# A chunked state recurrence with two token-mixing layers behind it: engine order of the recurrence written by hand, padded partitions, loads cut in pieces

## The chip, the cores and the metric

One core of one Trainium2 chip. The metric is the device time of one launch in microseconds, taken as the median of three runs; beside it stands one profiled execution with its own time.

## The reference, cut to what matters

Three layers run one after another. Only the first is touched here; the other two fill the second half of the time.

```python
B, H, S, D = 4, 8, 768, 40
state = zeros((B, H, D, D))
for t in range(S):
    y[:, :, t] = einsum('bhd,bhde->bhe', rt, state)
    Sa = einsum('bhde,bhe->bhd', state, at)
    state = state * wt[:, :, None, :] - einsum('bhd,bhe->bhde', Sa, bt)
    state = state + einsum('bhd,bhe->bhde', vt, kt)
x = y.transpose(0, 2, 1, 3).reshape(B, S, H * D)
x = moe(x)      # four causal attention experts, the best two of each token are mixed
out = moe2(x)   # a gated MLP with a matrix over the 768 tokens
```

All arithmetic is float32.

## The kernel before, in words

The 768 time steps are cut into 24 chunks of 32. `recurrence` handles one chunk per chain step `g`. Work on a chunk falls into three kinds.

Preparation, which doesn't depend on the state. `p_w(s)` is five VectorE operations on chunk `s`: a product scan of the decays (`pp`, L102), a reciprocal (L105), a scan backward (`rp`, L107), the scaled k and b (`kb`, L110) and the scaled a (`at`, L113); it ends with the load of chunk `s+3` (`load`, L85), since `xin` has three buffers. `p_t(s)` multiplies `kb` by `at` for two chunks at once on TensorE (L129) and VectorE masks the product out of PSUM (`ll`, L132). `p_x(s)` transposes `kb` on TensorE (L141, 8 operations) and ScalarE copies it out (`kbt`, L145).

Inversion, once for a unit of 2 or 4 chunks (`SIZES` = 2, 2, 4, 4, 4, 4, 4). `p_l` sends the masked products through memory into another layout (`lo`, L153, then `L`, L155), `p_sub` runs 31 pairs of VectorE operations on it (L168 and L170, each pair needs the one before), and `p_xt` sends the result back (`xo`, L176, then `xt`, L178). A unit has to be inverted before the first chain step of that unit can pass `f_u`.

The chain. Step `g` runs on TensorE `f_w` (L242, needs the state), `f_st` (state transposed, L287), `amat(g-1)` (L315), `f_kv` (L264), `f_u` (L253, needs `xt`), `ys(g-1)` (L332), `yk(g-1)` (L344, needs `am`), `f_s` (L272), `vt` (L297) and `f_lv(g+1)` (L235). VectorE adds to it `am` (L319), `xs` (L348) and the new state (L276, L280); ScalarE copies four results out of PSUM. The next `f_w` waits for L280.

What sets the order: the order of TensorE is that of the program text (`manual_schedule` names PE alone), and a table of numbers in `positions` says between which chain steps each piece of preparation is written. VectorE, ScalarE and the DMA queue of SyncE are ordered by a scheduler with its own estimate of times. PSUM tiles named `f` share two buffers (`FBQ = 2`); a tile takes a buffer when the reader of the last tile in it is done. They serve `p_t`, `p_x`, `f_st`, `amat`, `ys`/`yk` and `vt`.

Every load is one SyncE DMA (`xin` two): `xin` and `rv` have 104 partitions, two groups of 40 channels at partitions 0 and 64. The layers behind the recurrence (L394 on) and the preparation of their weights (`pre`) are the same in both kernels.

Of the kernel before, what the change touches and what calls it, by code (L numbers as in the profile page):

```python
# [23 lines left out]
AHEAD = 4.5  # L24
PPB = 11
RATB = 10
KTB = 11
FBQ = 2
PRQ = 2


def recurrence(ctx, tc, shape, x_in, rv_in, v_in, ident, store_x, pre=None):


    nc = tc.nc
# [7 lines left out]
    NW = NH * C  # L43

# [22 lines left out]
    ST = [cp.tile([Q, NH, 64], F32, name=f"ST{i}") for i in range(2)]
    U = [cp.tile([128, H, 64], F32, name=f"U{i}") for i in range(2)]
    for t in ST + U:
        nc.gpsimd.memset(t, 0.0)  # L70

    XIN, PP, AT, KBT, KB, LL, XT, RV, V = {}, {}, {}, {}, {}, {}, {}, {}, {}
    LX = {}
# [4 lines left out]
    def half(z, n=D):  # L78
        return slice(64 * z, 64 * z + n)

    def load(s):
        if s < NS:
            XIN[s] = ap.tile([Q, W + 3 * NW], F32, name="xin", bufs=3)
            for c0, c1 in ((0, W), (W, W + 3 * NW)):
                nc.sync.dma_start(XIN[s][:, c0:c1], x_in[s, :, c0:c1])  # L85

    def load_rv(g):
        if g < NS:
            RV[g] = cp.tile([Q, 4 * NW], F32, name="rv", bufs=2)
            nc.sync.dma_start(RV[g], rv_in[g])  # L90
# [6 lines left out]
    def p_w(s):  # L97

        xin = XIN[s]
        w = xin[:, :W]  # L100
        PP[s] = cp.tile([Q, NH, C + 1], F32, name="pp", bufs=PPB)
        nc.vector.tensor_tensor_scan(PP[s].rearrange("e n t -> e (n t)"), w[:, :W - 1],  # L102
                                     scan1.rearrange("e n t -> e (n t)"), 0.0, op0=OP.mult, op1=OP.add)
        inj = INJ[s % 2]
        nc.vector.reciprocal(inj[:, :, C:], PP[s][:, :, C:])  # L105
        rp = ap.tile([Q, NH, C + 1], F32, name="rp")
        nc.vector.tensor_tensor_scan(rp.rearrange("e n t -> e (n t)")[:, ::-1], w[:, 1:][:, ::-1],  # L107
                                     inj.rearrange("e n t -> e (n t)")[:, ::-1], 0.0, op0=OP.mult, op1=OP.add)
        KB[s] = ap.tile([Q, NH, 2, C], F32, name="kb", bufs=2)
        nc.vector.tensor_mul(KB[s], xin[:, W:W + 2 * NW].rearrange("e (n j t) -> e n j t", n=NH, j=2),  # L110
                             rp[:, :, None, 1:].to_broadcast([Q, NH, 2, C]))
        AT[s] = cp.tile([Q, NH, C], F32, name="at", bufs=RATB)
        nc.vector.tensor_mul(AT[s], xin[:, W + 2 * NW:].rearrange("e (n t) -> e n t", n=NH), PP[s][:, :, :C])  # L113
        load(s + 3)

    def p_t(s):

        k = unit_of[s]
        c = s - starts[k]
        if c == 0:  # L120
            LL[k] = cp.tile([128, 2, 4 * H, C], F32, name="ll", bufs=3)
        pt = ps.tile([128, 2, 512], F32, name="f", bufs=FBQ)
        pz = pt.rearrange("p z (c h t) -> p z c h t", c=2, h=H)
        for j in range(2):
            for h in range(H):
                for q2 in range(2):
                    for z in range(2):
                        n = 2 * h + q2
                        nc.tensor.matmul(pz[64 * q2:64 * q2 + 64, z, j, h],  # L129
                                         KB[s + j][half(z), n].rearrange("e j t -> e (j t)"), AT[s + j][half(z), n],  # L130
                                         start=(j == 0 and h == 0), stop=True, skip_group_check=True)
        nc.vector.tensor_mul(LL[k][:, :, c * H:(c + 2) * H], pt.rearrange("p z (n t) -> p z n t", t=C),  # L132
                             mask[:, None, None, :].to_broadcast([128, 2, 2 * H, C]))

    def p_x(s):

        KBT[s] = cp.tile([128, 2, H, D], F32, name="kbt", bufs=KTB)
        kb = KB[s].rearrange("e (h q) j t -> e h (q j t)", q=2)
        pt = ps.tile([128, 2, 512], F32, name="f", bufs=FBQ)
        for h in range(H):  # L140
            nc.tensor.transpose(pt[:, h // 4, h % 4 * Q:(h % 4 + 1) * Q], kb[:, h], ident[:Q, :Q])  # L141
        for g in range(2):
            src = pt[:, g, :4 * Q].rearrange("p (h e) -> p h e", h=4)
            for z in range(2):
                nc.scalar.copy(KBT[s][:, z, 4 * g:4 * g + 4], src[:, :, half(z)])  # L145

    def p_l(k):
# [4 lines left out]
        for q in range(4):  # L152
            nc.sync.dma_start(lo[q], LL[k][rows(q ^ 1), q % 2, :n])  # L153
        for q in range(4):
            nc.sync.dma_start(L[q * n:(q + 1) * n], lo[q].rearrange("j n t -> n j t"))  # L155
# [4 lines left out]
    def p_sub(k, j0, j1):  # L160
        L, X = LX[k]
        m_ = 4 * SIZES[k] * H
        L, X = L[:m_], X[:m_]
        for j in range(j0, j1):
# [5 lines left out]
            nc.vector.tensor_sub(X[:, :m, j + 1:], X[:, :m, j + 1:], tv)  # L170

    def p_xt(k):
# [7 lines left out]
    def positions(k):  # L180
        g, cs = starts[k], SIZES[k]
        steps = range(g, g + cs)
        if k == 0:
            at, l, sub, xt = [-100.0, -99.0], -98.5, (-90.0, -60.0), -59.0
        elif k == 1:
            at, l, sub, xt = [-98.0, -97.0], -96.5, (-2.0, 4.4), 4.5
        elif k == 2:
            at, l, sub, xt = [-20.0, -19.0, -1.9, 0.6], 1.1, (1.5, 10.2), 10.3
        elif k == 3:
            at, l, sub, xt = [2.6, 4.2, 5.9, 8.0], 11.4, (12.0, 22.0), 22.2  # L190
        else:
            at = [3 * (g - AHEAD - cs + c) for c in range(cs)]
            l, sub, xt = 3 * (g - 4.2), (3 * (g - 4.0), 3 * (g - 0.7)), 3 * (g - 0.6)
        out = []
        for c, s in enumerate(steps):
            out.append((at[c], p_w, s))
            if c % 2:
                out.append((at[c] + 0.3, p_t, s - 1))
            out.append((at[c] + 0.6 + (c + 1) % 2 * 0.05, p_x, s))
        out.append((l, p_l, k))  # L200
        for j in range(0, C - 1):
            out.append((sub[0] + (sub[1] - sub[0]) * j / (C - 1), p_sub, k, j, j + 1))
        out.append((xt, p_xt, k))
        return out

    when = sorted([x for k in range(len(SIZES)) for x in positions(k)], key=lambda x: x[0])

    def run_until(gap):
        while when and when[0][0] < gap:
            x = when.pop(0)  # L210
            x[1](*x[2:])

    order = ctx.enter_context(tc.manual_schedule(engines={mybir.EngineType.PE}))
    for s in range(3):
        load(s)
    load_v(0)
    load_rv(0)
    load_v(1)
    load_rv(1)
    run_until(0)  # L220

    QS = range(4)
    pw, wsb = {}, {}
    aq = {}
# [32 lines left out]
    def f_kv(g):  # L257
        aq["s"] = pS = ps.tile([128, 2, 512], F32, name="ps")
        flat = KBT[g].rearrange("p z h e -> p (z h e)")
        for h in range(H):  # L260
            for q in QS:
                z = q % 2
                n, o = (D, (H + h) * D) if z else (64, h * D)
                nc.tensor.matmul(pS[half(z, n), q // 2, h * D:(h + 1) * D], flat[rows(q), o:o + n], V[g][rows(q), h],  # L264
                                 start=(h == 0), stop=False, skip_group_check=True)

    def f_s(g):
        pS = aq["s"]
# [801 lines left out]
```

## Time and profile before

| what | us |
|---|---|
| median of three runs | 1202.46 (1192.55, 1202.46, 1209.99) |
| profiled execution, its own time | 1195.38 |
| its span, first to last instruction | 1193.3 |
| PE, DVE, ACT busy in the span | 899.8, 698.4, 379.7 |
| state of chunks 4, 8, 12, 16 complete | 214.7, 315.5, 420.4, 518.8 |
| first load of the second layer landed, end of the recurrence's part | about 654.5 |

PE is TensorE, PEld its weight loads, DVE VectorE, ACT ScalarE, SP or SPq SyncE and its DMA queue. A float32 matmul of the program appears as two matmuls and two weight loads in the trace. A wait named "issue" is time in which the engine waited for nothing that the profile shows.

### The profile page before, as it was taken

The page shows a single profiled execution, that of the slowest core. Times are in us where ns is not written, and L with a number is a line of the kernel's source. Part 1 is how long each engine was busy: PE and PEld are TensorE (multiplying, and loading weights), DVE is VectorE, ACT ScalarE, POOL GpSimd, SP SyncE. Part 2 cuts the span into 40 slices and gives each one's busy share as a digit, 9 for nine tenths or more (in the row PEclk, how much of TensorE's full clock was granted, in tenths as well). Part 3 has the DMA queues.
Part 4 walks back from the last instruction along what each step waited for, and adds up shares of the span by engine and source line. Part 5 has one row for each costly group of instructions (what it writes and reads, how often), then busy time and mean ns, then how long its engine had stood idle before and what let it go on. Part 6 is the DMA issues. An engine that isn't in the chain of part 4 may idle for free.

```text
span 1193.3 us, 38319 instructions
## 1 busy us (share of the span) xinstructions
PE 899.8 (75%) x17018; PEld 805.7 (68%) x17018; DVE 698.4 (59%) x1645; ACT 379.7 (32%) x1095; POOL 151.4 (13%) x278
## 2 busy tenths in 40 slices
PE   2354475776488377559897678789988998899988
PEld 2344464776477276548786556678987998799888
DVE  5788955626543842651111999786578556855650
ACT  1011011111111011101111568655565556555631
POOL 2000000000000000000000772012111211121131
PEclk9999999985555665655655679899999999999999
DMA  7645354535345233533332420100010001000000
GB/s 187 141 100 113 88 114 94 130 91 131 79 99 132 51 84 76 107 83 73 64 74 56 139 84 28 34 1 1 18 50 1 1 18 51 1 1 18 17 1 34
DMA packets 108462, 79.44 MB, mean 67 GB/s; under 512 B 88905, under 2 KB 95305, under 8 KB 105802
## 3 DMA queue, kind: packets, MB, share of 16 engines
q1 hardware_dynamic: 108298, 77.01, 27.8%
q8 instruction: 133, 2.18, 0.8%
q14 instruction: 31, 0.25, 0.1%
HBM read 62.83 MB, written 14.16 MB: 65 GB/s over the span
## 4 chain that ended last, share of the span: by engine, by line
PE 51%; DVE 27%; DMA 10%; issue 6%; ACT 4%; SPq 1%; POOL 1%; DVEq 0%; ACTq 0%; POOLq 0%
DVE sub L168 5%; DVE X L170 5%; DMA xin<-in_x_dram 5%; PE mm L827 5%; PE mm L828 4%; PE mm L829 4%; PE f L332 3%; PE f L315 3%; PE mp L786 3%; PE ps L264 3%; PE mp L716 2%; PE f L287 2%; PE pu L253 2%; PE f L344 2%; PE pw L242 2%
## 5 line engine op out<-in xcount | busy, mean ns | idle before, releaser
L141 PE MATMUL f<-ident,kb 104*128 104x104 f32 x192 | 38.0, 373 | 84.1 <-DVE ll L132 42.7
L168 DVE TENSOR_TENSOR sub<-X,L 128x31 f32<-128x31 f32 (+28 forms) x217 | 73.3, 338 | 44.1 <-DMA L<-lo 37.9
L141 PEld LDWEIGHTS f<-ident,kb 104*128 104x128 f32 x192 | 30.4, 213 | 87.0 <-DVE ll L132 43.6
L348 DVE TENSOR_TENSOR xs<-f,pp 104x512 f32<-104x512 f32 x24 | 16.6, 690 | 113.1 <-PE f L344 113.1
L756 ACT ACTIVATE f<-sc,nm 128x512 f32<-128x512 f32 (+3 forms) x128 | 68.9, 543 | 36.2 <-DVE nm L751 17.6
L477 DVE TENSOR_TENSOR ptl<-mp,pth 128x256 fp32r<-128x256 f32 (+2 forms) x144 | 65.4, 461 | 24.9 <-ACT pth L476 22.9
L170 DVE TENSOR_TENSOR X<-X,sub 128x31 f32<-128x31 f32 (+28 forms) x217 | 73.2, 337 | 6.2
L302 ACT COPY rv<-f 104x256 f32<-104x256 f32 x48 | 15.5, 375 | 192.4 <-PE f L297 187.3
L751 DVE TENSOR_REDUCE nm<-sc 128x1 f32<-128x512 f32 (+3 forms) x128 | 63.0, 502 | 23.4 <-PE sc L749 20.3
L319 DVE TENSOR_TENSOR am<-f,mask 128x512 f32<-128x512 f32 x24 | 16.5, 689 | 99.6 <-PE f L315 99.6
L145 ACT COPY kbt<-f 128x160 f32<-128x160 f32 x96 | 21.1, 307 | 165.7 <-PE f L141 165.7
L476 ACT CAST pth<-mp 128x256 fp32r<-128x256 f32 (+2 forms) x144 | 57.3, 410 | 35.1 <-PE mp L786 24.4
L786 PE MATMUL mp<-ident,f 128*128 128x128 f32 x336 | 61.0, 301 | 6.8 <-DVE ptl L477 3.8
L795 PE MATMUL pa<-pth,vv 128*128 128x256 f32 x192 | 55.8, 304 | 11.4 <-DVE at L807 8.2
L242 PE MATMUL pw<-ST,at 40*32 40x40 f32 x1536 | 30.3, 254 | 41.0 <-DVE ST L280 34.1
L129 PE MATMUL f<-at,kb 40*64 40x32 f32 x1536 | 47.4, 292 | 17.2 <-issue 14.2
L129 PEld LDWEIGHTS f<-at,kb 40*64 40x64 f32 x1536 | 45.1, 221 | 19.2 <-issue 15.8
L344 PE MATMUL f<-am,kbt 64*40 64x32 f32 x1536 | 36.9, 253 | 27.2 <-DVE am L319 23.6
L242 PEld LDWEIGHTS pw<-ST,at 40*32 40x32 f32 x1536 | 26.0, 154 | 46.1 <-DVE ST L280 36.1
L797 PE MATMUL pa<-ptl,vv 128*64 128x256 f32 x192 | 52.3, 294 | 2.2 <-DVE ptl L477 1.6
L344 PEld LDWEIGHTS f<-am,kbt 64*40 64x40 f32 x1536 | 32.9, 170 | 28.7 <-DVE am L319 24.1
L786 PEld LDWEIGHTS mp<-ident,f 128*128 128x128 f32 x336 | 43.8, 154 | 12.3 <-DVE f L772 4.1
(211 smaller groups left out, 2570.6 us busy)
## 6 DMA issues: line engine op xcount, KB each, us to landing
rv<-in_rv_dram SPq DMA_DIRECT2D x24, 832.0 KB
xin<-in_x_dram SPq DMA_DIRECT2D x24, 624.0 KB
xin<-in_x_dram SPq DMA_DIRECT2D x24, 214.9 KB
v<-in_v_dram SPq DMA_DIRECT2D x24, 160.0 KB
xd<-xs SPq DMA_DIRECT2D x96, 40.0 KB
out_dram<-ob SPq DMA_DIRECT2D x24, 160.0 KB
lo<-ll SPq DMA_DIRECT2D x20, 128.0 KB
L<-lo SPq DMA_DIRECT2D x20, 128.0 KB
```

The lines of the kernel that those rows point to most:

```text
L129: nc.tensor.matmul(pz[64 * q2:64 * q2 + 64, z, j, h], KB[s + j][half(z), n].rearrange("e j t -> e (j t)"), AT[s + j][half(z), n], start=(j ...
L141: nc.tensor.transpose(pt[:, h // 4, h % 4 * Q:(h % 4 + 1) * Q], kb[:, h], ident[:Q, :Q])
L168: nc.vector.tensor_mul(tv, X[:, :m, j:j + 1].to_broadcast([m_, m, n]), L[:, j:j + 1, j + 1:].to_broadcast([m_, m, n]))
L170: nc.vector.tensor_sub(X[:, :m, j + 1:], X[:, :m, j + 1:], tv)
L242: nc.tensor.matmul(pw[g][rows(q), h], AT[g][half(q % 2), n], ST[g % 2][half(q % 2), n, :D], start=False, stop=True, skip_group_check=True)
L344: nc.tensor.matmul(py[half(z), q2, c:c + C], KBT[g][64 * q2:64 * q2 + 64, z, 2 * p + h], am[64 * q2:64 * q2 + 64, h, z * HP + p], start=Fa ...
L476: nc.scalar.copy(hi, src)
L477: (lo_eng or nc.vector).tensor_sub(lo, src, hi.bitcast(F32))
L751: nc.vector.tensor_reduce(nm[:, z:z + 1], sc[:, :nn], op=OP.max, axis=AX.X, negate=True)
L756: nc.scalar.activation(pe[:, n0:n0 + nn], scs[z][:, :nn], AF.Exp, bias=nm[:, :1], accum_out=sm[:, z, i - i0:i - i0 + 1])
L786: nc.tensor.transpose(pp[:, j, z * 128:(z + 1) * 128], pes[z][:, (j0 + j) * 128:(j0 + j + 1) * 128], ident)
L827: nc.tensor.matmul(ps_, ah, bh, start=first, stop=False)
```

## The change

The order of VectorE and ScalarE is now that of the program text too, and the text is rewritten for it. `lazy(s)` holds the five VectorE operations of a chunk, `sub_parts(k)` the 31 pairs of a unit, `p_ll(s)` the masking, now of one chunk. `period(k)` lists the side work that is dealt out during the chain steps of unit `k`: the chunks of unit `k+2`, between them thirds of the pairs of unit `k+1`, each `p_ll` one chunk behind. In each chain step `fill` issues that list up to 52%, 86% and 100% of the step's share, at three places of VectorE's order: ahead of `am`, of `xs` and of the new state. TensorE's `p_t` and `p_x` come from a queue `pq` at two places of the step, after `yk` and after `f_lv`. The first four chunks and the pairs of unit 0 stand ahead of the chain, without anything between them.

The two channel groups are padded to 64 rows each, so `xin` and `rv` have 128 partitions; contractions over 40 rows become 64 rows with zeros, and the weights of `f_kv` are 40 columns wide where half were 64. `ps` is one tile for all steps, cleared once. Loads are cut: `xin` in four pieces, `rv` in four. ScalarE's copies of `kbt` and of the transposed state are two instead of four each.

Names in rows: `f`, `ps`, `pw`, `pu` are PSUM tiles, the number behind a name tells one tile from the next. VectorE before, in chain step g=3, where the pairs of unit 2 run, around that step's new state (`ST`):

```order
L348 TENSOR_TENSOR xs_2201<-f_2136,pp_252 104x512
L168 TENSOR_TENSOR sub_3224<-X_2319,L_2318 128x231
L102 SCALAR_TENSOR_TENSOR pp_2569<-xin_1533,scan1_86 104x528
L170 TENSOR_TENSOR X_2319<-X_2319,sub_3224 128x21x11
L105 RECIPROCAL INJ1_90<-pp_2569 104x16
L113 TENSOR_TENSOR at_2576<-xin_1533,pp_2569 104x512
L168 TENSOR_TENSOR sub_3227<-X_2319,L_2318 128x220
L107 SCALAR_TENSOR_TENSOR rp_2572<-xin_1533,INJ1_90 104x528
L170 TENSOR_TENSOR X_2319<-X_2319,sub_3227 128x22x10
L276 TENSOR_TENSOR ST0_93<-ps_2057,ST1_94 104x2x8x40
L110 TENSOR_TENSOR kb_2574<-xin_1533,rp_2572 104x1024
L168 TENSOR_TENSOR sub_3337<-X_2319,L_2318 128x207
```

VectorE now, in chain step g=5, from the new state on:

```order
L308 TENSOR_TENSOR ST0_124<-ps_132,ST1_125 128x2x8x40
L310 TENSOR_TENSOR ST0_124<-ST0_124,pp_724 128x2x8x40
L196 TENSOR_TENSOR sub_3206<-X_2302,L_2301 128x252
L198 TENSOR_TENSOR X_2302<-X_2302,sub_3206 128x18x14
L196 TENSOR_TENSOR sub_3209<-X_2302,L_2301 128x247
L198 TENSOR_TENSOR X_2302<-X_2302,sub_3209 128x19x13
L196 TENSOR_TENSOR sub_3212<-X_2302,L_2301 128x240
L198 TENSOR_TENSOR X_2302<-X_2302,sub_3212 128x20x12
L158 TENSOR_TENSOR ll_3215<-f_2565,mask_116 128x2x256
L118 SCALAR_TENSOR_TENSOR pp_3217<-xin_2249,scan1_111 128x528
```

The state stood inside a run of 62 pair operations and the next chunk's preparation; now three pairs stand between it and the mask of chunk 12 (`ll`, reading `f_2565`), and at most seven in a row anywhere in a four-step unit.

TensorE before, in chain step g=4, from `yk` on:

```order
L344 MATMUL f_2493<-am_2412,kbt_370 40x32 x32
L129 MATMUL f_2585<-at_2223,kb_2221 64x32 x32
L129 MATMUL f_2585<-at_2576,kb_2574 64x32 x32
L272 MATMUL ps_2414<-U0_95,kbt_496 40x40 x32
L297 MATMUL f_2690<-ident_60,U0_95 128x128 x4
L235 MATMUL pw_2697<-v_2262,ll_522 32x40 x32
L141 MATMUL f_2731<-ident_60,kb_2574 128x104 x8
L242 MATMUL pw_2697<-ST1_94,at_517 32x40 x32
```

TensorE now, at the same place of g=5; `f_2565`, the `p_t` product of the chunk before, was written one chain step earlier:

```order
L368 MATMUL f_2880<-am_2844,kbt_824 40x32 x32
L147 MATMUL f_2950<-at_2830,kb_2834 64x32 x32
L303 MATMUL ps_132<-U1_127,kbt_1134 40x40 x32
L325 MATMUL f_3035<-ident_60,U1_127 128x128 x4
L272 MATMUL pw_3042<-v_2654,ll_1000 32x40 x32
L170 MATMUL f_3076<-ident_60,kb_2834 128x104 x8
```

One chunk's `p_t` stands where two stood, and it takes a buffer of `f` while the one of the chunk before still holds another.

SyncE's queue at the start, from the eleventh row on, before:

```order
L85 DMA xin<-in_x_dram 104x529
L85 DMA xin<-in_x_dram 104x1536
L85 DMA xin<-in_x_dram 104x529
L85 DMA xin<-in_x_dram 104x1536
L85 DMA xin<-in_x_dram 104x529
L85 DMA xin<-in_x_dram 104x1536
L153 DMA lo_227<-ll 32x512 x4
L85 DMA xin<-in_x_dram 104x529
L85 DMA xin<-in_x_dram 104x1536
L155 DMA L<-lo_227 16x32x32 x4
```

And now, after the same three chunks, `v` and `rv`:

```order
L69 DMA xin<-in_x_dram 128x529
L69 DMA xin<-in_x_dram 128x512 x3
L69 DMA xin<-in_x_dram 128x529
L69 DMA xin<-in_x_dram 128x512 x3
L181 DMA lo_257<-ll 32x512 x4
L183 DMA L<-lo_257 16x32x32 x4
```

Two chunks instead of three stand ahead of `lo` of unit 0, and none between `lo` and `L`.

The diff, cut to its core:

```diff
-    def half(z, n=D):
+    def half(z, n=64):
-            XIN[s] = ap.tile([Q, W + 3 * NW], F32, name="xin", bufs=3)
-            for c0, c1 in ((0, W), (W, W + 3 * NW)):
+            XIN[s] = ap.tile([128, W + 3 * NW], F32, name="xin", bufs=3)
+            for c0, c1 in ((0, W), (W, W + NW), (W + NW, W + 2 * NW), (W + 2 * NW, W + 3 * NW)):
                 nc.sync.dma_start(XIN[s][:, c0:c1], x_in[s, :, c0:c1])
-            nc.sync.dma_start(RV[g], rv_in[g])
+            for c in range(4):
+                nc.sync.dma_start(RV[g][:, c * NW:(c + 1) * NW], rv_in[g, :, c * NW:(c + 1) * NW])
-    order = ctx.enter_context(tc.manual_schedule(engines={mybir.EngineType.PE}))
+    order = ctx.enter_context(tc.manual_schedule(engines={mybir.EngineType.PE, mybir.EngineType.DVE,
+                                                          mybir.EngineType.Activation}))
...
+    def period(k):
+        subs = sub_parts(k + 1) if k + 1 < len(SIZES) else []
+        steps = range(starts[k + 2], starts[k + 2] + SIZES[k + 2]) if k + 2 < len(SIZES) else []
+        out = []
+        n = max(len(steps) - 1, 1)
+        for i, s in enumerate(steps):
+            out += lazy(s)
+            out += subs[len(subs) * i // n:len(subs) * (i + 1) // n]
+            if i:
+                out.append((0.69, lambda s=s - 1: p_ll(s)))
+        if steps:
+            out.append((0.69, lambda s=steps[-1]: p_ll(s)))
+        else:
+            out += subs
+        return out
...
-                n, o = (D, (H + h) * D) if z else (64, h * D)
-                nc.tensor.matmul(pS[half(z, n), q // 2, h * D:(h + 1) * D], flat[rows(q), o:o + n], V[g][rows(q), h],
+                nc.tensor.matmul(pS[half(q % 2, D), q // 2, h * D:(h + 1) * D], KBT[g][rows(q), q % 2, h],
...
+        def fill(frac):
+            while dq and done[0] + dq[0][0] / 2 <= total * frac + 1e-6:
+                t, f = dq.pop(0)
+                done[0] += t
+                f()
+
+        for g in range(starts[k], starts[k] + SIZES[k]):
+            i = g - starts[k]
+            at = [(i + x) / SIZES[k] for x in SEG]
+            f_w(g)
+            f_st(g)
+            if g:
+                amat(g - 1)
+            if not last:
+                f_kv(g)
+            fill(at[0])
+            if g:
+                am(g - 1)
+            f_u(g)
+            if g:
+                ys(g - 1)
+                yk(g - 1)
+                load_rv(g + 1)
+            pe()
+            fill(at[1])
+            if g:
+                xs(g - 1)
+            if not last:
+                f_s(g)
+            load_v(g + 2)
+            vt(g)
+            f_lv(g + 1)
+            pe(1 if len(pq) < 3 else 2)
+            fill(at[2])
+            if not last:
+                state(g)
```

## Rows read from the trace of the kernel before

**Rows 1.** Stretches: busy time of PE, PEld, DVE, ACT, POOL; clock, DMA share, GB/s.

```profile
0.00:214.70 214.70, 99.60 (x2840) 89.31 (x2840) 153.61 (x325) 22.20 (x85) 10.52 (x26) 1.00 0.53 117
20.00:30.00 10.00, 0.00 (x0) 0.00 (x0) 1.71 (x3) 0.19 (x1) 0.00 (x0) 1.00 0.83 196
214.70:518.80 304.10, 204.96 (x7144) 184.93 (x7144) 155.26 (x316) 37.93 (x140) 3.87 (x10) 0.63 0.44 96
518.80:654.50 135.70, 115.28 (x4192) 104.34 (x4192) 25.76 (x40) 18.94 (x64) 0.00 (x0) 0.53 0.34 73
654.50:1193.30 538.80, 479.93 (x2842) 427.08 (x2842) 363.78 (x966) 300.65 (x806) 137.01 (x242) 0.93 0.09 28
```

**Rows 2.** What PE waited for, 214.7 to 518.8: total, times, longest.

```profile
PE f L344 <- DVE am L319: 18.4, 3, 8.1
PE pw L242 <- DVE ST L280: 16.8, 5, 5.4
PE f L141 <- DVE xs L348: 16.4, 2, 9.0
PE f L129 <- issue: 10.1, 6, 3.7
...
PE f L315 <- issue: 1.0, 2, 0.8
```

**Rows 3.** Timeline, all engines, 276 to 340 (start, length, idle before).

```profile
286.34 0.19 DVE L168 TENSOR_TENSOR sub<-X,L 128x31 f32<-128x31 f32 x1 [8.25 <-DMA L<-lo]
...
309.21 1.65 PE L141 MATMUL f<-ident,kb 104*128 104x104 f32 x8 [7.40 <-DVE xs L348]
...
314.63 0.82 DVE L280 TENSOR_TENSOR ST<-ST,pp 104x640 f32<-104x640 f32 x1
...
315.50 1.29 PE L242 MATMUL pw<-ST,at 40*32 40x40 f32 x64 [4.64 <-DVE ST L280]
```

**Rows 4.** Timeline of the start, 0 to 112.

```profile
0.79 2.71 SPq L85 DMA_DIRECT2D xin<-in_x_dram  x6
...
28.23 1.26 DVE L102 TENSOR_TENSOR_SCAN pp<-xin,scan 104x528 f32<-104x528 f32 x1 [8.86 <-DMA xin<-in_x_dram]
...
33.66 1.20 DVE L132 TENSOR_TENSOR ll<-f,mask 128x1024 f32<-128x1024 f32 x1
...
47.79 0.17 DVE L168 TENSOR_TENSOR sub<-X,L 64x31 f32<-64x31 f32 x1
```

**Rows 5.** Chain of waits, two stretches: start, length, what.

```profile
93.49 3.04 DMA xo<-X
96.55 5.74 DMA xt<-xo
...
275.56 6.86 DMA lo<-ll
282.44 3.78 DMA L<-lo
```

**Rows 6.** One stretch with the five VectorE operations of one chunk, columns of rows 1.

```profile
330.40:335.00 4.60, 1.73 (x63) 1.60 (x58) 4.44 (x5) 0.00 (x0) 0.00 (x0) 0.50 0.63 116
```

**Rows 7.** Costliest groups: line, engine, count, then busy and mean ns of one.

```profile
L168 DVE TENSOR_TENSOR sub<-X,L 128x31 f32<-128x31 f32 (+28 forms) x217 | 73.3, 338 | 44.1 <-DMA L<-lo 37.9
...
L170 DVE TENSOR_TENSOR X<-X,sub 128x31 f32<-128x31 f32 (+28 forms) x217 | 73.2, 337 | 6.2
...
L319 DVE TENSOR_TENSOR am<-f,mask 128x512 f32<-128x512 f32 x24 | 16.5, 689 | 99.6 <-PE f L315 99.6
```

**Rows 8.** Timeline of one chain step without side work, 549 to 586.

```profile
555.38 0.87 ACT L292 COPY s<-f 104x160 f32<-104x160 f32 x4 [1.07 <-PE f L287]
...
557.16 1.94 PE L264 MATMUL ps<-v,kbt 32*64 32x40 f32 x64
...
559.02 1.29 PE L253 MATMUL pu<-wsb,xt 32*32 32x40 f32 x64
```

**Rows 9.** Code fetches of 214.7 to 518.8: packets, MB, share of 16 engines.

```profile
q8 instruction: 56, 0.92, 1.4%
```

More of the change, by code (lines that the diff above doesn't have):

```diff
@@ L106, in p_w @@
[L106 to L111, printed above, removed]
@@ L176, in p_xt @@
         nc.sync.dma_start(xo.rearrange("q n l t -> (q n) (l t)"), LX[k][1][:4 * n].rearrange("n l t -> n (l t)"))
-        for q in range(4):
+        for q in QS:
             nc.sync.dma_start(XT[k][rows(q), :n], xo[q].rearrange("n l t -> l n t"))
[L180 to L190, printed above, removed]
-        else:
[L192 to L203, printed above, removed]
-        return out
@@ L206, in recurrence, with lazy, first @@
[L206 to L211, printed above, removed]
-    order = ctx.enter_context(tc.manual_schedule(engines={mybir.EngineType.PE}))
[L214 to L224, printed above, removed]
+    def lazy(s):
+        parts = []
+        def first():
+            parts.extend(w_parts(s))
+            parts[0][1]()
+        return [(1.25, first)] + [(t, lambda i=i: parts[i][1]()) for i, t in ((1, 0.9), (2, 1.25), (3, 1.22))]
@@ L353, in recurrence @@
     prep = None
     f_lv(0)
-    for g in range(NS):
-        last = g == NS - 1
-        f_w(g)
-        f_st(g)
-        amat(g - 1)
-        if not last:
-            f_kv(g)
-        run_until(3 * g + 1)
-        f_u(g)
-        ys(g - 1)
-        yk(g - 1)
-        load_rv(g + 1) if g else None
-        run_until(3 * g + 2)
-        if not last:
-            f_s(g)
-        load_v(g + 2)
-        vt(g)
-        f_lv(g + 1)
-        run_until(3 * g + 3)
-        if not any(x[1] in (p_w, p_t, p_x) for x in when) and prep_stack is not None:
+    for k in range(len(SIZES)):
+        dq = period(k)
+        total = sum(t for t, _ in dq)
+        done = [0.0]
+        def fill(frac):
+            while dq and done[0] + dq[0][0] / 2 <= total * frac + 1e-6:
+                t, f = dq.pop(0)
+                done[0] += t
+                f()
+        for g in range(starts[k], starts[k] + SIZES[k]):
+            i = g - starts[k]
+            at = [(i + x) / SIZES[k] for x in SEG]
+            last = g == NS - 1
+            f_w(g)
[25 more added lines that the diff above has]
+                state(g)
+            if prep is not None:
+                for _ in range(QPR):
+                    next(prep, None)
+        while dq:
+            dq.pop(0)[1]()
+        while pq:
+            pe()
+        if k == len(SIZES) - 3:
@@ L375, in recurrence @@
             prep_stack.close()
[L376 to L377 removed]
+        if k == len(SIZES) - 2:
             sub_stack.close()
[L379 removed]
             prep = pre() if pre is not None else None
[L381 to L383 removed]
     amat(NS - 1)
+    am(NS - 1)
     ys(NS - 1)
     yk(NS - 1)
+    xs(NS - 1)
     if prep is not None:
```

241 lines of the change are left out of this document (133 added, 108 removed).

## The prediction

> **What bounds the kernel now.** I read the stretches first, cut at the chain steps that complete a unit [rows 1]. Behind 654.5 us TensorE is busy 479.9 of 538.8 us; that code isn't touched, and I leave the stretch as it is. In the recurrence no engine is full: up to 214.7 VectorE works 153.6 us and TensorE 99.6; in the next twelve steps TensorE 205.0 of 304.1; in the last eight 115.3 of 135.7. So the gain has to come out of waits. Second view: what TensorE waited for in the twelve steps [rows 2]. `am`, the new state and `xs` cost 51.6 us in 10 waits, up to 9.0 each; nine rows of "issue", from 10.1 down to 1.0, add 40.7. Third, the timeline of one unit's worst step [rows 3]. VectorE takes up the pairs at 286.34 and stays with them; `xs` held back TensorE's next group by 7.4 us, the state is finished at 315.45 and `f_w` follows at 315.50. Those 29 us belong to one of four steps that take 101 together (304.1 / 3). Last, the start [rows 4]: VectorE has the product of chunks 0 and 1 to mask but was ordered to wait 8.86 us for chunk 3 first; `ll` runs at 33.66, the first pair at 47.79, and further chunks are mixed into the pairs, so the result leaves at 93.49 and lands at 102.29 [rows 5].
>
> **The start and the first four steps.** A chunk is 4.7 us of VectorE (4.44 in five operations and their gaps [rows 6]), an inversion 31 x (0.338 + 0.337) = 20.9 and 22.2 with gaps, `am`, `xs` or a one-chunk `ll` 0.69 each [rows 7], a state 1.65 (two of 0.82 [rows 3]).
>
> `lo` of unit 0 now leaves at about 18, but stands behind five chunks and two `rv`. Today the first part of chunk 3 is in at 28.2 [rows 4]; its rest and chunk 4, 1.5 MB at 196 GB/s, take 7.6 more, `lo` then 2.4 and `L` with its issue 5 (both estimates, from 6.86 and 3.78 under load [rows 5]): 43.2. This assumes that a load takes as long as now. Today's load rate is 196 GB/s with 0.83 of 16 engines busy [rows 1]. If that total is the limit, 128 rows for 104 cost 23% more time, and the pairs start at 52; if DMA cost nothing, VectorE's four chunks still hold them to about 24. I stay at 43.2, nearest to today's 47.79.
>
> On the engines, the busy share of 0.83 is nearly 13/16. [...] In the row six issues take 2.71 us while their data need more than ten [rows 4], so issue runs ahead of the data and I add nothing; in series, 16 further issues ahead of `lo` would add about 7 us.
>
> Then VectorE alone sets the pace. Unit 0's pairs run to 65.2. `xo` and `xt` take another 9 (3.04 + 5.74 [rows 5]), so `f_u(0)` can start at 74 instead of 102, and VectorE has the next unit's work meanwhile. The first two units hold two chain steps each and the side work of a four-chunk unit: twice 4 x 4.7 + 22.2 + 4 x 0.69 is 87.6; four states, three `am`, three `xs` are 10.7; together 98.3. Three waits are added, because VectorE is now strictly in order. At the end of each of the two units, the last `kb` has to go through TensorE's `p_t` and back before the two `ll` and the state behind them: TensorE has `p_x`, `f_s`, `vt`, `f_lv`, `p_t`, `p_x`, `p_t` to do after `xs`, and VectorE idles about 6 us, twice. And the first pair of unit 2 waits for `L`: the round trip from `ll` is about 11 (6.86 + 3.78 and an issue [rows 5]), of which VectorE has filled 6: 5 more. With 2.6 for handovers the sum is 65.2 + 98.3 + 12 + 5 + 2.6 = 183, against 214.7: **32 saved**.
>
> **The next twelve steps.** TensorE is the longer engine here (per unit 68.3 of work against VectorE's 51.8 [rows 1]). `f_kv` loses its wide weights: 1.94 becomes about 1.29, the same count with 32 columns [rows 8]; that is 2.5 per unit, 65.8 stay. The zero rows cost nothing: VectorE's time goes by columns (`am` on 128 rows and `xs` on 104 both took 0.69). What takes the place of the 17.2 us of VectorE waits per unit? I went through the new order of TensorE and VectorE by hand. With two `f` buffers a `p_t` product holds one until its `ll`, and `ll` is a whole chunk behind.
> - Second step: both buffers hold products. `vt` stands behind `f_s` and gets one when VectorE has done the state (1.65), three pairs (2.6) and `ll` (0.69): 4.9 us. Behind `vt` wait `f_lv`, `p_x` and the next `f_w`.
> - Fourth step: `f_st` waits for seven short pairs and `ll` behind the state (5.1); `p_t` and `f_w` cover all but 2.7.
> - With one buffer free, `amat` waits for ScalarE's copy of `f_st` (0.87 [rows 8]) in three steps, and `p_t` or `p_x` for `xs` in two: 2.7 + 1.8.
> - First step: `am` stands behind two pairs that wait for `L`, which lands 9 us into the step; `yk` is late by 2.2, `vt` by 0.5.
> - End of the unit: the last `ll` and the state take 2.5, `p_x` (1.65 [rows 3]) covers most: 0.9.
>
> That is 15.7, so the waits are spread more than removed. Handovers stay at 2.3 (101.4 less 68.3, 17.2 and 13.6). The issue waits are 13.6 per unit now. Code fetches (56 packets, 4.7 per step [rows 9]) go through the same DMA engines as the loads; a TensorE that waits for a buffer lets its code catch up, so I take 9.7, between nothing and 20. A unit: 65.8 + 15.7 + 2.3 + 9.7 = 93.5, three 280.5: **24 saved**. If `L` came 5 us later, the first step would lose those 5.
>
> **The last eight steps** have no `p_t`, no chunks, and the pairs of one unit only. `f_kv` gives 8 x 0.6 back, the wait for the last `L` takes about 2, and the weights of the second layer, now split at fixed places of VectorE's order, up to 3 when their load is late: 136. ScalarE's fewer, longer copies move the same columns: nothing.
>
> **Sum.** 183 + 280.5 + 136 + 538.8 = 1138.3 of span, 1140.4 with the 2.1 around it, against 1195.38 for the profiled execution. That execution lies 7.1 under the median of the runs; the same shift gives 1147.
>
> **Rivals.**
> 1. *More is hidden.* The buffer waits cover all code fetches and the loads run freer: three units of 83.8 (29 less) and a start 19 earlier: 1099. For it: a fetch that is late by up to 3.7 [rows 2] fits into a buffer wait of 4.9. Against: fetches fall late where loads are in flight, and loads now come closer together.
> 2. *The loads are bound by bytes.* 196 GB/s stays while `xin` and `rv` grow by 23%: the start is 9 later, `L` and `xt` come some 2 us later at six places, and issue waits grow to 17 per unit: 9 + 8 + 22 more, 1186. For it: the start's flat 196 GB/s. Against: 0.83 of the engines, so three hardly took part. The change would then not do what it says of the loads.
> 3. *Code fetch is slower, and the kernel with it.* [...] Price: 4.7 fetches a step over 20 steps is 94 fetches. Slower than before by 2%, 1226.5, needs 80 more than my sum, so 0.85 us more on each fetch; at 1 us it is 1241. For it: TensorE's issue waits of up to 3.7. Against: today's issue waits are 0.7 a fetch (40.7 / 56) with the DMA engines 0.44 busy; they would have to more than double.
>
> **How the numbers follow.** Forecast 0.57, with 1115 to 1178 as its own range (issue waits 0 to 20 per unit, pairs from 40 to 50); rival 1 0.22, rival 2 0.14, rival 3 0.07. A measurement tells about 2% from no change: 1178 and 1226. Faster: all of the forecast but its edge, and rival 1, 0.78; the same: mostly rival 2, 0.15; slower: rival 3, 0.07. The range, 1088 to 1190, leaves rival 3 and the outer ends out.
>
> **What would show it.** Right: `f_u(0)` near 74; the state of chunk 4 complete near 183, of chunk 16 near 464; no step of 35 us; in each four-step unit a `vt` that waits about 5 us for VectorE's `ll` and an `f_st` that waits about 3; VectorE idle for `L` at unit starts. Wrong: `vt` without a wait (then the units go towards 83), issue waits above 20 per unit, or the first pair after 50. If the part behind the recurrence differs from 538.8 by more than 10, the premise that it stays fails.

## The result, and the profile after

The changed kernel takes 1111.37 us, median of 4 runs (1109.5 to 1122.17), against 1201.22 for the kernel before, of 4 runs beside it: 0.927 of its time, 95% interval 0.918 to 0.936. The profiled execution takes 1109.5 us, with a span of 1107.8.

The stretches after, cut at the same chain steps as [rows 1] and with the same columns, and below them two pieces of 5 us:

```profile
0.00:165.10 165.10, 90.56 (x2832) 80.30 (x2832) 133.35 (x276) 19.35 (x49) 12.80 (x27) 0.66 0.55 158
165.10:433.20 268.10, 183.31 (x7152) 162.73 (x7152) 155.93 (x306) 36.09 (x96) 3.56 (x8) 0.65 0.49 129
433.20:569.00 135.80, 98.09 (x4192) 86.80 (x4192) 49.76 (x110) 18.02 (x48) 0.75 (x3) 0.70 0.41 97
569.00:1107.80 538.80, 480.06 (x2842) 427.24 (x2842) 365.52 (x966) 300.91 (x806) 138.32 (x242) 0.93 0.09 28
...
215.00:220.00 5.00, 4.16 (x217) 3.78 (x208) 0.98 (x2) 1.38 (x4) 0.00 (x0) 0.85 0.03 7
235.00:240.00 5.00, 4.16 (x124) 3.77 (x127) 1.58 (x3) 1.10 (x3) 1.11 (x2) 0.50 0.61 160
```

These rows show where the 85.5 us of span went: 49.6 from the start and the first four steps (214.7 to 165.1), 36.0 from the next twelve (304.1 to 268.1), nothing from the last eight (135.7, now 135.8) or behind. And a thing that the prediction did not have: TensorE does its matmuls in less busy time, 183.3 us in the twelve steps for 205.0 before, 98.1 in the last eight for 115.3, though these last still take as long. The zero rows make 18.5 and 16.0 us of that, as an experiment below shows; the narrower weights of `f_kv`, which the prediction had, belong to the rest. The granted clock there is 0.65 and 0.70; the clock records of this trace and of the one before hold two values alone, 0.5 and 1.0, called the low and the high level from here on. In the two short pieces TensorE is busy 4.16 us each, but runs 217 matmuls in the one and 124 in the other. The 1.00 of the first two lines of [rows 1] is no granted clock: the trace of the kernel before holds no clock record before 254.4 us, and the view prints 1.00 where there is none. The 64 matmuls of `f_kv` took 1.94 us there at 116.7, as they did at the low level in [rows 8]. The lines from 10 to 20 us further down have their 1.00 for the same reason.

What TensorE waited for in the twelve steps, answering to [rows 2] (total, times, longest):

```profile
PE f L325 <- DVE ll L158: 14.9, 3, 5.0
PE f L358 <- issue: 10.5, 8, 2.2
...
PE f L341 <- ACT s L320: 7.6, 9, 0.8
...
PE f L368 <- DVE am L347: 4.7, 1, 4.7
PE pw L279 <- DVE ST L310: 3.9, 3, 1.5
...
PE f L317 <- DVE ll L158: 1.2, 1, 1.2
```

Of the big waits for `am`, the state and `xs`, 51.6 us in all, one for `am` of 4.7 is left and small ones of up to 1.5; the largest is now `vt` (L325), once a unit. All waits for other engines add up to 37.4 us (51.6 before), all rows of "issue" to 47.2 (40.7 before). Four lines of the timeline answer to [rows 3] and [rows 4]: the first pair, `f_u(0)`, and twice the 64 matmuls of `amat`, once at the high and once at the low clock level.

```profile
30.49 0.18 DVE L196 TENSOR_TENSOR sub<-X,L 64x31 f32<-64x31 f32 x1 [0.40 <-DMA L<-lo]
...
58.57 0.31 PE L290 MATMUL pu<-wsb,xt 32*32 32x40 f32 x2 [20.11 <-DMA xt<-xo]
...
217.78 1.15 PE L341 MATMUL f<-rv 64*64 64x32 f32 x64 [0.84 <-ACT s L320]
...
237.25 1.96 PE L341 MATMUL f<-rv 64*64 64x32 f32 x64 [0.84 <-ACT s L320]
```

The start moved most: the first pair runs at 30.49 (47.79 before), because the chunks are there sooner.

What "issue" stands for can be read from the same trace, from the times of the 16 KB packets of the queue that the view calls `q8 instruction`, taken here for TensorE's code. Here are the next three issue waits of that stretch:

```profile
222.21 0.84 PE L358 MATMUL f<-rv,s 64*64 64x32 f32 x49 [1.46 <-issue]
...
227.03 1.16 PE L303 MATMUL ps<-U,kbt 32*40 32x40 f32 x52 [2.63 <-issue]
...
232.58 1.02 PE L147 MATMUL f<-at,kb 64*64 64x32 f32 x56 [1.95 <-issue]
```

Code packets landed at 220.83, 225.70 and 231.06, so TensorE went on 1.4, 1.3 and 1.5 us after each. In the twelve and the last eight steps all 37 issue waits over 1 us end 1.2 to 1.6 us after a code packet has landed; of the nine equally long waits for other engines, one does. So these issue waits are waits for code. The twelve steps have 14304 matmuls and weight loads on 56 packets, 255 to a packet.

### The profile page after: what moved, and what is told of

Read it like the earlier page. It is cut to its first block, busy times and chain, and to the rows that moved or that the text cites. A ratio compares the mean times of both kernels' runs of the same rounds, so it can differ in the third digit from the quotient of the medians.

```text
span 1107.8 us, 38413 instructions
## 1 busy us (share of the span) xinstructions
PE 852.0 (77%) x17018; PEld 757.1 (68%) x17018; DVE 704.5 (64%) x1657; ACT 374.4 (34%) x999; POOL 155.4 (14%) x279
## 4 chain that ended last, share of the span: by engine, by line
PE 53%; DVE 18%; issue 9%; ACT 5%; DMA 4%; SPq 1%; POOL 0%; ACTq 0%; DVEq 0%; POOLq 0%
PE mm L880 5%; PE mm L881 5%; PE mm L882 4%; PE mp L839 3%; PE f L341 3%; PE mp L769 2%; PE f L358 2%; PE f L317 2%; PE f L147 2%; PE ps L303 2%; PE pw L272 2%; PE f L368 2%; PE pw L279 2%; PE f L325 2%; PE f L170 2%
## 5 line engine op out<-in xcount | busy, mean ns | idle before, releaser
L196 DVE TENSOR_TENSOR sub<-X,L 128x87 f32<-128x87 f32 (+27 forms) x217 | 73.4, 338 | 33.4 <-DMA L<-lo 27.8
L198 DVE TENSOR_TENSOR X<-X,sub 128x87 f32<-128x87 f32 (+27 forms) x217 | 73.8, 340 | 7.4
L330 ACT COPY rv<-f 128x256 f32<-128x256 f32 x48 | 15.5, 375 | 175.7 <-PE f L325 159.3
L147 PE MATMUL f<-at,kb 64*64 64x32 f32 x1536 | 43.0, 272 | 30.2 <-DVE kb L133 13.8
L147 PEld LDWEIGHTS f<-at,kb 64*64 64x64 f32 x1536 | 39.4, 196 | 34.0 <-issue 11.5
L347 DVE TENSOR_TENSOR am<-f,mask 128x512 f32<-128x512 f32 x24 | 16.5, 689 | 69.9 <-PE f L341 69.9
L374 DVE TENSOR_TENSOR xs<-f,pp 104x512 f32<-104x512 f32 x24 | 16.5, 688 | 58.7 <-PE f L368 53.0
L172 ACT COPY kbt<-f 128x320 f32<-128x320 f32 x48 | 18.1, 429 | 99.4 <-PE f L170 99.4
L848 PEld LDWEIGHTS pa<-pth,vv 128*128 128x128 f32 x192 | 39.1, 203 | 17.2 <-DVE at L860 9.6
L290 PE MATMUL pu<-wsb,xt 32*32 32x40 f32 x1536 | 27.9, 231 | 29.6 <-DMA xt<-xo 22.2
L184 POOL MEMSET X<- 128x1024 f32 (+1 forms) x7 | 6.6, 951 | 312.9 <-DMA xo<-X 312.9
L292 ACT COPY U<-pu 128x320 f32<-128x320 f32 x24 | 10.2, 426 | 118.6 <-PE pu L290 118.6
```

Of the source, the lines that this page charges most:

```text
L147: nc.tensor.matmul(pt[64 * q2:64 * q2 + 64, z, h * C:(h + 1) * C], KB[s][half(z), n].rearrange("e j t -> e (j t)"), AT[s][half(z), n], sta ...
L196: nc.vector.tensor_mul(tv, X[:, :m, j:j + 1].to_broadcast([m_, m, n]), L[:, j:j + 1, j + 1:].to_broadcast([m_, m, n]))
L848: nc.tensor.matmul(pa[:, c0:], vv[:, j0 + j, e].rearrange("p a h -> p (a h)"), pth[:, j, c0:], start=(j0 + j == 0), stop=False, skip_group ...
```

## The experiments

My theory after the result was that order, loads and zero rows each carry a part: the order removes the long waits, 128-row loads arrive sooner, and the zero rows raise TensorE's clock, whose gain is given back as issue waits. The kernel before took medians of 1196 to 1199 beside these runs. Two versions that are 1% apart are not told apart by the 95% intervals of their ratios, which overlap; where the text leans on a difference of some 10 us, the four times of each don't overlap and the stretches of the profiled executions show it too. Where a kernel's stretches are shown, they are the twelve steps and the last eight, up to the last `xs` (133.9 us before, 133.7 after, counted so), with the columns of [rows 1].

**Two halves: the order alone, and all but the order.** The first is the changed kernel with the 104-row layout, products over 40 rows and whole loads:

```
-    C, Q = 32, 128
+    C, Q = 32, 104
-            XIN[s] = ap.tile([128, W + 3 * NW], F32, name="xin", bufs=3)
+            XIN[s] = ap.tile([Q, W + 3 * NW], F32, name="xin", bufs=3)
...
```

> The new order alone: 104 rows everywhere, products over 40 rows, whole loads, as in the kernel before. Theory A, order, loads and zero rows each carry a part: the first pair near 43 as foretold with loads as they were (12 us later than after the change), TensorE at the low clock, 1135 to 1145. Theory B, the order carries nearly all: 1111 to 1118. Theory C, loads and rows carry most: 1165 to 1190.

Measured: 1142.06 us (1135.18 to 1147.55), 0.956 of before (0.947 to 0.966); the first pair at 38.1, 5 us earlier than theory A has it, the state of chunk 4 at 181.8.

```profile
181.80:456.60 274.80, 203.37 (x7152) 181.22 (x7152) 156.27 (x307) 36.18 (x97) 3.54 (x8) 0.57 0.48 106
456.60:600.90 144.30, 111.98 (x4192) 100.26 (x4192) 49.85 (x110) 18.02 (x48) 0.75 (x3) 0.55 0.39 81
```

The other is the kernel before with 128 rows, products over 64 rows and loads in pieces:

```
-    C, Q = 32, 104
+    C, Q = 32, 128
-                                     KB[s + j][half(z), n].rearrange("e j t -> e (j t)"), AT[s + j][half(z), n],
+                                     KB[s + j][half(z, 64), n].rearrange("e j t -> e (j t)"), AT[s + j][half(z, 64), n],
...
```

> The kernel before with everything but the order: 128 rows, products over 64 rows, loads in pieces. Theory A, each carries a part: the granted clock rises above 0.5 in the recurrence, but the long waits for VectorE stay, 1170 to 1185. Theory B, the order carries nearly all: 1195 to 1203. Theory C, loads and rows carry most: 1130 to 1150.

Measured: 1164.02 us (1161.64 to 1170.39), 0.976 (0.967 to 0.984); the state of chunk 4 at 192.5. Its twelve steps, and its waits there:

```profile
192.50:493.00 300.50, 194.66 (x7144) 174.75 (x7144) 155.53 (x316) 38.15 (x140) 3.88 (x10) 0.60 0.43 111
...
PE f L345 <- DVE am L320: 21.0, 3, 8.0
PE f L142 <- DVE xs L349: 17.5, 2, 9.0
PE pw L243 <- DVE ST L281: 15.5, 4, 5.4
```

Theory A's time holds for the order alone; for this half its direction does, but 1164 lies 6 us under its range (and 14 above C's). The order is worth 57 us of 1199, all else 35, both together 88: they hardly overlap. By stretch, the start became 33 us shorter with the order alone, 22 with the rest and 50 with both, the twelve steps 29, 4 and 36. The waits of [rows 2] stay as they were without the new order (54 us), so it is the order that removes them. What this cut doesn't part: the narrow weights of `f_kv`, ScalarE's merged copies and the `p_t` of one chunk went with the order.

**The zero rows.** Products over 40 rows, all else as after the change:

```
-                                     KB[s][half(z), n].rearrange("e j t -> e (j t)"), AT[s][half(z), n],
+                                     KB[s][half(z, D), n].rearrange("e j t -> e (j t)"), AT[s][half(z, D), n],
...
```

> The changed kernel with the matrix products over 40 rows as before (each half of 64 without its 24 zero rows); loads, layout and order stay. Theory A, the zero rows raise the granted clock of TensorE: in the 268 us of twelve steps the clock goes from 0.65 back towards 0.50 and TensorE's busy time from 183 up to about 200, in the last eight steps from 98 to about 115; since part of that time is spent on issue waits today, the kernel loses 8 to 20 us, 1120 to 1131. Theory B, the denser order raises the clock: clock and busy time stay, 1111 within 5.

Measured: 1115.16 us (1113.94 to 1117.32), 0.935 (0.925 to 0.944).

```profile
166.20:433.30 267.10, 201.77 (x7152) 179.84 (x7152) 156.02 (x307) 36.08 (x96) 3.55 (x8) 0.56 0.49 129
433.30:567.60 134.30, 114.14 (x4192) 102.09 (x4192) 49.76 (x110) 18.02 (x48) 0.75 (x3) 0.54 0.41 97
```

The mechanism of theory A is there, its price is not. The clock falls to 0.56 and 0.54 and TensorE's work grows by 18.5 and 16.0 us; the stretches take as long as with zero rows. What gives way are the issue waits: 30.2 us in the twelve steps for 47.2, 16.3 in the last eight for 31.6; those over 1 us are 20 for 37, and all 20 end 1.2 to 1.7 us after a code packet. So with the loads in pieces the clock's gain is given back almost whole, to waits for code. With whole loads it is not quite so:

> Loads whole, of 128 rows, with products over 40 rows: between the order alone (1142) and whole loads with 64 rows (1100). Theory A, the gain between these two comes from the loads' 128 rows, and the clock's share is taken back by issue waits: 1100 to 1108, TensorE at the low clock (0.54 in the last eight steps, busy 112 to 114). Theory B, it is the clock's: 1125 to 1140.

(The edits of this run are those of the run above and the next one together.) Measured: 1111.8 us (1106.1 to 1113.59), 0.927 (0.922 to 0.933).

```profile
165.20:432.10 266.90, 195.62 (x7152) 173.86 (x7152) 155.97 (x306) 36.06 (x96) 3.09 (x7) 0.58 0.47 128
432.10:565.50 133.40, 114.46 (x4192) 102.32 (x4192) 49.80 (x111) 18.01 (x48) 1.04 (x4) 0.53 0.39 99
```

The time lies 4 us above theory A's range and 13 under B's; A's clock and busy time hold within 1 us. Against the order alone the 128 rows of the loads give 30 us (1142 to 1112), or 26 against the other version with loads of 104 rows below (1137.56), some 16 of them in the start (state of chunk 4 at 165.2 for 181.8). The products over 64 rows give another 11 (1112 to 1100, next run): 30 us less of TensorE's work shorten the twelve and the last eight steps by 14. Theory A's ordering holds.

**The pieces.** Loads whole, of 128 rows:

```
-            for c0, c1 in ((0, W), (W, W + NW), (W + NW, W + 2 * NW), (W + 2 * NW, W + 3 * NW)):
+            for c0, c1 in ((0, W), (W, W + 3 * NW)):
...
-            for c in range(4):
-                nc.sync.dma_start(RV[g][:, c * NW:(c + 1) * NW], rv_in[g, :, c * NW:(c + 1) * NW])
+            nc.sync.dma_start(RV[g], rv_in[g])
```

> The changed kernel with its loads whole again: a chunk in two pieces and r, v in one, of 128 rows. Theory A, the pieces bring the faster start: the first pair goes from 30.5 back to about 37 and the kernel loses 5 to 8 us. Theory B, the 128 rows (16 engines) alone do it: first pair at 30 to 32, 1111 within 4.

Measured: 1100.31 us (1099.36 to 1102.4), 0.922 (0.915 to 0.929): faster than the changed kernel, which neither theory had. The first pair runs at 28.96, so theory B's start holds.

```profile
168.80:427.30 258.50, 185.97 (x7152) 164.69 (x7152) 156.27 (x306) 36.11 (x97) 3.53 (x8) 0.64 0.47 129
427.30:555.50 128.20, 94.23 (x4192) 83.34 (x4192) 49.75 (x110) 18.03 (x48) 0.76 (x3) 0.73 0.40 102
```

The pieces cost 11 us in all: 9.6 and 5.5 in the later stretches, where 8 and 3 us of issue waits go with them. Up to chunk 4 they look 3.7 us better (165.1 for 168.8), but four other versions with whole loads take 162.6 to 167.3 to there, so no gain is shown; the first pair is 1.5 later with pieces, since `lo` is issued at 19.58 for 16.77. With products over 40 rows the pieces cost only 3 us (1115.16 to 1111.8, above) and the stretches are alike, so this price belongs to the faster TensorE.

> The changed kernel with only r, v whole (one load of 1 MB for four of 256 KB); the chunks stay in four pieces. Theory A, the pieces of r, v cost: the last eight steps take 128 as with all loads whole and not 133.7, the twelve steps 258 to 262, and the start stays at 165: 1096 to 1101. Theory B, the chunks' pieces cost: 1107 to 1113.

Measured: 1103.79 us (1099.3 to 1104.34), 0.921 (0.915 to 0.926); the twelve steps take 263.1, the last eight 128.7, the start 166.2. Nearer to theory A, 3 us above its range: r and v hold most of the price. Why pieces of 256 KB cost stays open: a code packet takes 0.98 us (median of the two stretches) with pieces as with whole loads.

**The wait for `ll`.** On top of whole loads, `ll` is masked right behind the next chunk's operations:

```
             out += lazy(s)
+            if i:
+                out.append((0.69, lambda s=s - 1: p_ll(s)))
             out += subs[len(subs) * i // n:len(subs) * (i + 1) // n]
-            if i:
-                out.append((0.69, lambda s=s - 1: p_ll(s)))
```

> Whole loads, and besides each chunk's ll is masked right behind the next chunk's five operations, before the pairs, so that a buffer f comes free about 2.6 us to 17 us earlier. Theory A, the wait of vt and f_st for ll (14.9 and 2.6 us in the twelve steps) is on the path: it goes, the twelve steps take 258.5 less about 13, the kernel 1100 less 10 to 15. Theory B, the supply of instructions paces TensorE: the waits for ll go, and the issue waits grow from 39 by as much; the kernel stays within 4 of 1100.

Measured: 1089.84 us (1085.81 to 1092.86), 0.911 (0.904 to 0.917); the twelve steps take 249.9. Its largest waits there:

```profile
PE ps L302 <- issue: 13.5, 5, 4.3
PE f L357 <- issue: 11.6, 7, 3.4
PE f L367 <- issue: 8.2, 5, 2.9
```

Both theories have a part. The `vt` wait is gone (2.7 us for `ll` are left, at `amat`) and waits for other engines fall by 17.5 us (32.3 to 14.8), but issue waits grow by 12 (39.2 to 51.1): of a removed wait about half reaches the time (258.5 to 249.9).

**Code supply.** First whether the loads delay it:

```
+        if 12 <= g < NS:
+            RV[g] = RV[g - 2]
-        if g < NS:
+        elif g < NS:
```

> Whole loads, but from chunk 12 on r and v aren't loaded: the tiles of two chunks before are used again, so these chunks' outputs are computed from other r and v. About 12 MB of loads less, most of them beside the last eight steps. Theory A, code fetches are late because loads stand in the same queues: in the last eight steps the issue waits go from 28 to under 12, the steps from 15 to 17 us to 13 to 14, the kernel is 12 to 20 faster than 1100. Theory B, a fetch has a pace of its own of about 3.3 us: issue waits stay above 22, steps at 15 to 16, the kernel within 6 of 1100.

Measured: 1092.34 us (1089.2 to 1095.05), 0.912 (0.907 to 0.917).

```profile
427.60:549.00 121.40, 92.60 (x4192) 81.38 (x4192) 49.72 (x110) 18.01 (x48) 0.75 (x3) 0.75 0.24 47
```

Traffic is halved (47 GB/s for 102), issue waits are still 24.8 for 28.3, steps 14.0 to 16.5. Nearer to theory B, with 2 us more gain than it allows. From the start times of the instruction queue's 16 KB packets, the shortest interval between two code fetches in the last eight steps is 3.34 us after the change, 3.28 with whole loads and 3.33 here: less traffic leaves it where it was. In the changed kernel's trace a packet takes a median 0.98 us, TensorE goes on no sooner than 1.19 after it has landed, and no packet starts sooner than 1.06 after such a restart: by estimate 3.2 in all, if each leads to the next. Then with fewer instructions, on whole loads and early `ll`. V and U share a tile, so that one product over 64 rows does what `f_kv` and `f_s` did:

```
-            V[g] = cp.tile([128, H, D], F32, name="v", bufs=2)
+            V[g] = cp.tile([128, 2, H, D], F32, name="v", bufs=2)
...
+            for q in QS:
+                nc.scalar.copy(V[g][rows(q ^ 1), q % 2], pu[rows(q ^ 1)])
...
-                nc.tensor.matmul(pS[half(q % 2, D), q // 2, h * D:(h + 1) * D], KBT[g][rows(q ^ 1), q % 2, h],
-                                 U[g % 2][rows(q ^ 1), h, :D], start=False, stop=True, skip_group_check=True)
+                nc.tensor.matmul(pS[half(q % 2, D), q // 2, h * D:(h + 1) * D], KBT[g][half(q // 2), q % 2, h],
+                                 V[g][half(q // 2), q % 2, h], start=(h == 0), stop=True, skip_group_check=True)
...
-            if not last:
-                f_kv(g)
```

> Whole loads, ll early, and besides the 64 matmuls of f_kv in each step are gone: V and U lie in one tile so that f_s multiplies 64 rows of both at once. 128 of about 1200 TensorE instructions a step less, 0.5 code fetch; ScalarE makes four small copies more per step, beside ys and yk. Theory A, code supply paces TensorE: about 12 of 110 fetches less at 3.4 to 4.4 us each, 1089.8 less 30 to 45, the last eight steps (125.8) take 112 to 116. Theory B, TensorE's work paces it: 0.8 to 1.3 us a step less, the last eight steps 116 to 121, the kernel less 15 to 28. Theory C, the chain of engines paces it, and f_kv lay beside the chain: within 6 of 1089.8, or slower by the copies, up to 20.

Measured: 1054.31 us (1052.27 to 1059.03), 0.884 (0.877 to 0.891), the fastest version of this study.

```profile
162.60:390.10 227.50, 161.65 (x6384) 143.20 (x6384) 155.60 (x306) 56.14 (x145) 3.14 (x7) 0.70 0.54 149
390.10:508.50 118.40, 88.48 (x3744) 78.81 (x3744) 49.57 (x110) 29.70 (x76) 0.99 (x4) 0.69 0.43 110
```

The same stretches of the version before it, with early `ll`:

```profile
165.40:415.30 249.90, 182.90 (x7152) 162.54 (x7152) 156.31 (x307) 36.17 (x97) 3.50 (x8) 0.66 0.49 137
415.30:541.10 125.80, 94.44 (x4192) 83.46 (x4192) 49.75 (x111) 18.01 (x48) 0.81 (x3) 0.73 0.41 104
```

35.5 us less: within theory A, above B's 15 to 28, and C falls. But the last eight steps, 118.4, lie in B's range and not in A's. And the run doesn't part the two: up to the last `xs` TensorE's busy time falls by 31 us (`f_kv` alone was busy for 26), nearly the 33 that this part is shorter, while in the two stretches issue waits fall by 15 and waits for other engines grow by 12. That supply and not work sets the pace rests on the code packets and on the zero rows, where 35 us of work alone cost at most 4; this run agrees with it.

**Which property of the load.** The order alone once more, with loads of the first 104 of 128 rows, and with loads of 112:

```
-                nc.sync.dma_start(XIN[s][:, c0:c1], x_in[s, :, c0:c1])
+                nc.sync.dma_start(XIN[s][:, c0:c1], x_in[s, :104, c0:c1])
...
-    C, Q = 32, 104
+    C, Q = 32, 128
```

> The order alone, but its loads take the first 104 of 128 rows of arrays laid out with 128: the same bytes per load as before the change, other start addresses. In the traces a packet of 8 KB takes 583 to 601 ns with 104 rows and 309 with 128. Theory A, the number of rows (13 of 16 DMA engines) makes the packets slow: 8 KB stays near 580 ns, the first pair near 38, 1137 to 1147. Theory B, where a chunk's data start makes them slow: 8 KB near 310 ns, first pair near 30, 1108 to 1118.

> The order alone with loads of 112 rows, 8 more than needed; the engines work on 104 rows as before. Theory A, only a load that all 16 engines share is fast (112 rows are 14 or 16 engines by 8 or 7 rows): if 16 engines with 7 rows each carry it, 8 KB takes near 310 ns and the kernel 1108 to 1120; if 14 carry it, 8 KB stays at 450 to 600 ns and the kernel at 1130 to 1150. Theory B, start addresses: between the two, 8 KB at 310 to 600 ns without a set pattern.

Measured: 1137.56 us (1134.54 to 1140.91), 0.951 (0.947 to 0.955), for 104 of 128 rows, and 1120.15 (1114.83 to 1124.13), 0.936 (0.930 to 0.942), for 112. The stretch from 10 to 20 us after the start; the last two numbers are DMA share and GB/s. The order alone, 104 rows:

```profile
10.00:20.00 10.00, 7.02 (x144) 6.25 (x144) 7.78 (x12) 1.51 (x4) 0.36 (x3) 1.00 0.86 219
```

The first 104 of 128 rows:

```profile
10.00:20.00 10.00, 7.02 (x144) 6.25 (x144) 7.77 (x12) 1.51 (x4) 0.47 (x3) 1.00 0.85 206
```

Loads of 112 rows:

```profile
10.00:20.00 10.00, 6.60 (x139) 5.83 (x132) 7.77 (x11) 1.51 (x4) 0.93 (x3) 1.00 1.02 277
```

Loads of 128 rows, whole, with products over 40 rows:

```profile
10.00:20.00 10.00, 6.04 (x116) 5.27 (x112) 7.75 (x11) 1.51 (x4) 0.57 (x4) 1.00 1.03 411
```

The median 8 KB packet of the start took 583, 597, 480 and 309 ns in these four. Theory A of the first run holds, start addresses are out. In the second neither form of it does: 112 rows have a DMA share of 1.02, all 16 engines, and their packets are still 1.6 times as long as those of 128, so the number of engines alone isn't it. Nor is it the load's own rows alone: `v` has 128 rows in all of these, and its 1280-byte packets took a median 84 to 92 ns beside loads of 104 rows, 74 beside 112 and 55 beside 128. The time goes by the rows of the loads in flight; why, stays open. The last eight steps took 134.6 with 104 of 128 rows and 144.3 in the order alone with the same bytes, so that stretch of the order alone isn't to be leaned on.

## Why the prediction was right, and where it was not

The sign and the class were right. The median, 1111, lies 36 under the forecast and just under its own range of 1115 to 1178, inside the wide one. Of the span's 30.5 us, 17.9 are in the start, 12.4 in the twelve steps, 0.2 in the last eight.

- *"This assumes that a load takes as long as now"* is the step that failed. The first pair came at 30.5, not 43.2, `f_u(0)` at 58.6, not 74, chunk 4's state at 165.1, not 183. The order alone has loads of 104 rows as before: there chunk 4's state is at 181.8, near the 183 worked out under that assumption, though the pair, at 38.1, is 5 us early, so single terms of that sum were off and made up for each other. The DMA share is 0.83 before, nearly 13/16, and 1.05 after (below); in the same stretch the traces have 13 packets in flight at once for 70% of the time before, never fewer, and 16 or more for 99% of it after. What I missed is that the packets become faster: those of 2116 bytes, the first part of a chunk, took a median 87 ns in the first 30 us, for 135. The bound "if DMA cost nothing, about 24" held. Rival 2, loads bound by total bytes, is wrong: 384 GB/s where 191 were.

```profile
10.00:20.00 10.00, 6.19 (x141) 5.42 (x139) 7.85 (x10) 1.57 (x8) 0.00 (x0) 1.00 0.83 191
10.00:20.00 10.00, 7.02 (x144) 6.25 (x144) 7.77 (x11) 1.51 (x4) 0.28 (x3) 1.00 1.05 384
```

- *The pieces* I priced at nothing. Measured, 128 rows gave 26 to 30 us, and pieces of 256 KB cost 11 (3 with products over 40 rows). "Issue runs ahead of the data" held in the main: the pair is 1.5 us later with pieces, not 7.
- *The `vt` wait*, 4.9 foretold and 5.0 at most measured, and `amat` behind ScalarE, 2.7 a unit foretold and 2.5 measured, stand. `xs` held 1.7 (1.8). `f_st` was put at 2.7 a unit and took 0.4, `am` at 2.2 and took 1.6. All waits came to 12.5 a unit, for 15.7, and the 2.3 of handovers are not there.
- *"The zero rows cost nothing"* was true of the changed kernel's time and wrong of TensorE: they raise its clock (from 0.56 to 0.65 in the twelve steps), and a unit's work is 61.1 us instead of 65.8. With whole loads they are worth 11 us.
- *Issue waits*, 9.7 a unit foretold, are 15.7, inside the 0 to 20 that I gave. I argued that a TensorE that waits lets its code catch up; with early `ll` 17.5 us fewer of other waits did come with 12 more of issue. I missed the other direction: a TensorE that works faster waits for its code more (47.2 us in the twelve steps, 30.2 with products over 40 rows). Work and issue together are 76.8 for my 75.5: two errors that nearly cancel, which is luck. A unit took 92.3, 89.0 and 86.7, for 93.5.
- *The last eight steps*, 136 foretold, 135.8 measured, by luck and not for the reasons given: TensorE's work is 17 us less and the issue waits are 14 more (31.6 for 17.3).
- *Rival 1* had the start nearly right (19 earlier, measured 17.9) and the units wrong: they gave 12.4 of its 29 us, and the buffer waits did not hide the fetches, since issue waits grew beside them. *Rival 3*, slower code fetch, did not come about: 56 fetches in the twelve steps as before, and the shortest intervals are alike (3.41 us before, 3.40 after). A code packet took a median 1.23 us before when the loads' DMA share was over 0.5 meanwhile, 1.07 otherwise; after, 0.95 and 1.00. The pieces did cost, but not by slower fetches.

```profile
q8 instruction: 56, 0.92, 1.4%
```

That is the instruction queue of the changed kernel in the twelve steps (packets, MB, share), the same row as [rows 9]; the fastest version has 50 there.

## What to carry to other kernels

When a profile shows many short "issue" waits on TensorE, see whether they end behind code packets, and if so count its instructions before its work: here 35 us of added work cost at most 4 us with loads in pieces, 30 us cost 11 with whole ones, and merging two products into one over twice the rows gave 35. Try a load with all 128 rows, padded if need be, and whole; both paid here (128 rows 26 to 30 us; whole loads 11, or 3 with products over 40 rows). A wait that an order by hand removes is worth what the next limit leaves of it: about half, for `ll` (8.6 us of 17.5).

## What was not expected of the hardware

- A packet of 8 KB took a median 583 to 601 ns in loads of 104 rows, 480 in those of 112, 309 to 318 in whole loads of 128 rows.
- Zero rows in a product (64 rows for 40) moved the mean granted clock of the last eight steps from 0.54 to 0.69, with the same count of instructions: between the two values of the clock records, 0.5 and 1.0, that is by estimate 38% of the time at the higher one, for 8%. 64 matmuls of `amat` took 1.96 us at 0.5 and 1.15 at 1.0.
- Code fetches of 16 KB followed each other no closer than 3.2 us in the twelve and the last eight steps of any run here, at 47 GB/s of traffic as at 102. Of the 350 issue waits over 1 us there, in the 13 traces, 346 end 1.1 to 1.7 us after such a packet has landed.
